# Two layers of sliding-window attention and token MLP on one core: the MLP's first product cut in five parts, the last attention chunk halved, masks moved to GpSimd

## The chip, the cores and the metric

The kernel runs on one core of a Trainium2 chip. A core has five engines that run side by side and wait for each other through semaphores: TensorE (PE; its weight loads are shown apart as PEld), VectorE (DVE), ScalarE (ACT), GpSimd (POOL) and SyncE (SP), which here issues every DMA. The metric is the device time of one execution in microseconds; smaller is better. The times before come from three runs.

## The reference

The input is x, 2048 rows of 512 numbers in bf16. Two kinds of block alternate, each added to x, twice over:

```python
def _A_ref(x, wqkv, wo):                      # sliding-window attention
    H = 32; Dh = D // H; W = 256              # 32 heads of 16
    ...
    scores = jnp.einsum("bhqd,bhkd->bhqk", q, k) * (Dh ** -0.5)
    mask = (idx[:, None] - idx[None, :] >= 0) & (idx[:, None] - idx[None, :] < W)
    p = _softmax(jnp.where(mask[None, None], scores, -1e9), axis=-1)
    ...
def _B_ref(x, w1, b1, w2, b2):                # MLP over the rows (tokens)
    h = _layernorm(x, axis=-1)
    u = _gelu(jnp.einsum("bsd,sf->bdf", h, w1) + b1)      # F = 1792
    y = jnp.einsum("bdf,fs->bds", u, w2) + b2
    ...
x = x + _A_ref(_layernorm(x, axis=-1), A_wqkv, A_wo)
x = x + _B_ref(_layernorm(x, axis=-1), B_w1, B_b1, B_w2, B_b2)
x = x + _A_ref(...)
x = x + _B_ref(...)
```

Each row attends to itself and the 255 rows before it. The token MLP's first product sums over all 2048 rows, so its sum can be finished only when the last rows have left the attention.

## The kernel before

Everything lies in on-chip memory in tiles of 128 partitions: x is 16 row tiles of 128 rows (`x_sb`), its normalised form is `xh_sb`. The work is written down as a list of operations (`op`), each with its engine, what it reads and what it writes; `Graph` derives the dependences. The order in which each engine gets its operations is not that of the list: it is a fixed, precomputed sequence (`ORDER`, unpacked by `begin_order` and laid out by `replay`), which also picks for some operations one of several engines (`alts`). Within one engine's queue, work runs strictly in this order. Buffers come from pools (`Pool`, `Tile`): a tile is taken at its first use and given back after its last, so a pool's size decides how early a later operation may start. `emit` writes the waits.

**Attention** works on chunks of query blocks of 64 rows (`CHUNKS`, as first block and number of blocks). For a chunk of 8 blocks and each of four groups of eight heads it makes five score units (`attention_plan`), for a chunk of 4 blocks five units for two groups together, one of them joint. A score unit is a set of small products of queries and spread keys (L710, line names as in the profile), four at a time in four strips of the array; then two exponentials on ACT over 128 x 1024 numbers (L736), which write the probabilities `pt` (seven buffers); then the masks; then the product with the values (L774), which takes three units, or two, or all five, at once. The sums of four head groups are turned on DVE (L794), divided (L798, L800), turned back (L805), multiplied with `wo` (L534) and added to x (L816).

The masks are applied in two ways. In most units GpSimd multiplies the finished probabilities with 0 or 1, as bit patterns (L757, made in `f_mask`). In layer 0, for the units listed in `BIASED` (in the chunk (4,4) the units 0 and 1, in (8,8) and (16,8) the units 2 and 4), PE adds a large negative number to the scores ahead of the exponential, with further small products of a selection matrix `sel` and a table `bb` (L721); these two are built at the start by twelve operations on DVE (L465, L472).

**Projections**: `qkv` turns the normalised rows of a chunk of 512 rows (four row tiles), multiplies them with `wqkv` (L534) and copies the results out of the accumulators: queries to `qT` (two buffers), keys over `stg` to `kbd` (three buffers, each for all four head groups; every second strip of 16 must be zero, cleared at the start by POOL, L482), values over `vst` and a DMA to `vb`.

**Token MLP**: the first product is accumulated in parts over row tiles. `PARTS` of layer 0 lists row tiles 0 to 3 (in the list after chunk (8,8)) and 4 to 11 (after chunk (24,8)), each for all 14 column tiles of 128; `u_part` makes them (L534, weights `w1b`, four buffers loaded by SP, L830), and DVE or ACT copies the first part's sums out (L880, L882), DVE adds the second's (L884). The last part, row tiles 12 to 15, is made by `u_last` (L895) after the attention, with the addition of the earlier sums on DVE (L906) and the activation on ACT (L910). A part starts only when its last row tile is there. Then `y_block` makes the second product row tile by row tile (L534, weights in `pt` and `w2b`), and its result goes to x (L936); in layer 0 these row tiles feed layer 1's projections.

At the start, `f_warm` issues 42 products of no use on PE while x is on its way (L395); then come the layer norm of the first row tiles (L492, L494, L505, L512), their turning on PE (L570, copied out at L579) and the first projections.

Of the kernel before, what the change touches and what calls it, by code (L numbers as in the profile page):

```python
# [15 lines left out]
    'c-p;HKZx_l6(4zLzti5$7bY-;K9~!0puiNmpaTUI(18Lf6i^|84jgdd!Urx~xX^(L6)IG?Foy~k3aD_QfD02`nBc;N3kO`daIuApEnIA|#THv^v4x9_*WO+4'  # L16
    '?zeYelH;ELNSb*wn)iFZ_j?rAF$R-hFaQl1MD2Rqc6z-ObQ9Q0I+5N0tsfxQJZ;LS!FS>l^i3OrI;cSnFmiiGyf&@5jmh6O=dO2NTm8i)OK$V|W~Nxg7^#NJ'
    'jjxzWMnhGW85~ZB!%dnDi#TCwz^U3X`=CE6K9r;3hd+J&A?k2$x9mn-Z`d_2@O-X0ys9W)ZDu~_p3arkO4F#KBpQtoqCinF!l<RHmyDTgyH(T%p_c@!H#fEo'
    'NVc*z7gx)rZQEqE`f@g-o6U?;v>FcifYR~k?(U8nMQON*e0lM;b<<dPEWE%=X9dwLoN9=Vo17!WSnl--R;v{`8+g1d*>cJ3@O|9YvQTV@`f(kFjD=AUgsre$'
    'mjA9V@Th3F+et!`s7Pp0q!H~kBfshgxY=lUp55>Wvn;<FRI61LU0q#Y-QCqLYZ$k#WABm}OV6p{>GYd_jSO=bcu3bBr;09vC~|ja!lu#fqK=_h3gbLjuXRIT'  # L20
    'a!#pfo0flZVL8syS+3A~GSdksh!<QHCs)g&$TCEfZLfz>#~TpkdUG||B%9m2+h+6bE_+|=tk>7K7_G*e%|()&uk6*#j?BWIPUot6bv2)_*K2Q>=l1z>B&XKg'
    'DyRL~yx;HJqp?r^Zjx_F+3)wVtoP?$-ox0o`(-~>Rof^i<(RQv7KT|Cwma9?##N_f7`!dZ?W!Eqo6V-Gaxd@!cT|~DS=Togx=zl|?Un7?OUKb<O`D9@OKwg$'
    '?qil?Sx)`T_iKsZPm=VbJa==KQf6B`HlsMHitSt~JG!h9g`8o_rj#1mnrfOxu!7Gf>dus*pyxPd;&??bw|cg!&;-S?5ow{JzsFe9G4C}pzhS5}U?O*xYML_R'
    '8dE5vf`XLl(`koLQ*e|6?M|uHY8uyded}y3Sw7SC1u$>c*Yh==&mq(h!o$<S_U>*7Zjp>Jl7)3rC=5s-ALRKKH=ENe&+`%3&7?8_zQ3WWtI8m5M2;{Bk^ngl'
    'u$o#GL7@4_b2+yR1^@)8FvHAj119Rkvcv#&b;cFWn8J346i_Hu$1|92=?jbMq~kh{m{1W|VJu$GCON?XqtwsUIE&-Bu4z#fQ4JHMAm5K7U*KTbwp9fHdjbMV'
    'm&;26=ks%@Y4&(V`NSIIdn>*ITkt_fc^F1#XR_REbUFyir@DR`*6Xz(2&&)LzpmFcSckGqF?3zzpPtDO%!F+@EEl#lzj2)5(CO6DG_BRTjYit&h(c>Sx^8M7'
    'htT&_)3FTz08v#!bO0e&i6l#g$OIN%rb*E4?d>%}NM9@#=bMcHSJj7;;dwe9t0PSt2wV$I^RnFc7(36h)k-OUTmGZk{ZU~GpbE0JQ?=wWjO%rs>)%n4GNv*Y'
    'Lc6t+<;M3LzFfBX`U0>1fEJ6AfmuFSET@ZtF)%La7=UrJ2}bqls8$1kBfBekI9yD1IoC9)>}SFOj}XB)>-O&;>=#KQb)_uIFt)O!i_H<nol=i1p%7CTg;_Q0'
    'R<c$%%i19boodag1MYfGvs(2;O5JL;&W8hs*K0x|8jS5K%drEYKECS%lQ^cR_49K_t6C6ZHqrg*G`PGBdIcD(*Ur_|KQ->yg7K=U8pdW5U)WKkYjLcGmTQS3'
    'Y1ok+;?~ubt{M98&jG)^k^R43se(cm4O(9<mkUbgA|q{8`Jnu6P>x0;H*hDO=eW~yOrW#SEK!i<e7-39L=mLw!SPO_I-R2YvUibQ;=EVIdEmO^F&=l_K~|=e'  # L30
    'h6%<7fr!}k_%@Dx&#hkgLCaq{#72&72SH5;RW)l?P1p5=*t%{IP=D)r)Kgs7kY)Ws5RZrsQC(8gFm6Xw9y_)xi(Uu?J2g!)Wzb@A+<>9RDO6~k)l{|sz?*Kj'
    'TQr#f{n{ZIsVtYNyqGT~!Twn~o6g`VoQy@F(QpU`Vdy2jZjx2{{Z<jhu4Q$_TV$gnhwUKsyk@<oyKW^-JvWKH7)Hp}bwg+m)OEpco3_~*L`|+jRfdoPfe^%w'
    'wS{mxxfBm~7Tv5j&AhAteYMi<RVrGaZjHw0<Kb#)>3Ugy^G%)`gP~}g3P_5qAU}XMwBN^;l{gDG-^oeXj^fDr_FLcgEVOZb&oSjc8W2DNA)>SZLZ?PIK;j7l'
    'Qr1ghFHL|@tDV{aAbYckswh+eghG(brY&u}U5oM(!bJiy8YAH(8b#T!*TsLm=vxM8Hd{?SYBZV+N-zYnnYeM1c1$OAfnkV3HUiVqEV+PyF;T;YX%Wj7osI~x'
# [59 lines left out]
class Graph:  # L94
# [4 lines left out]
    def __init__(self, nc, es):  # L99
        self.nc = nc  # L100
        self.sem = {e: es.enter_context(nc.semaphore(f"s_{e}")) for e in self.ENGS}
        self.dsem = [es.enter_context(nc.semaphore(f"s_dma{i}")) for i in range(self.NDMA)]
        self.ops = []
        self.last_w = {}
        self.readers = {}

    def op(self, eng, fn, reads=(), writes=(), cost=200.0, prio=None, dma=False, after=(), holds=(), cfg=None, cls=None,
# [20 lines left out]
        for k in writes:  # L128
# [3 lines left out]
            for rd in self.readers.get(k, ()):  # L132
                deps[rd.idx] = rd
# [882 lines left out]
```

## Time and profile before

| what | value |
|---|---|
| median of three runs | 444.22 us (443.94 to 444.88) |
| the profiled execution | 445.56 us, its span 443.6 us |
| granted TensorE clock, mean | 0.996 |
| PE busy | 418.5 us, 94% of the span |
| ACT busy | 322.7 us, 73% |
| DVE busy | 307.4 us, 69% |
| POOL busy | 201.1 us, 45% |
| masks on POOL (L757) | 226 operations, 146.9 us |
| mask products on PE (L721) | 352, from 21.7 to 117.0 us |

A span is what the profile sees between first and last instruction. A line of a group gives line number, engine, operation, what it writes and reads, the number of instructions, busy time and mean duration in ns, and then the idle time of the engine ahead of them, with what ended it. A line of a timeline gives start, length, engine, line and operation, the number of instructions merged in it, and in brackets the idle time ahead. The stages lie in time as follows: first exponential at 11.1 us; layer 0's attention to about 161; the end of the token MLP's first product to about 186; second product and layer 1's first projections to about 205; layer 1's attention to about 362; its first product to 392 and its second to the end. PE pipelines its products, so the busy time of a product contains a drain that lies under the next.

### The profile page before, as it was taken

How to read it: one execution, taken by the hardware profiler on the slowest of the kernel's cores; microseconds unless marked ns; L12 is line 12 of the kernel's file. 1: busy time of each engine (PE TensorE's matmuls, PEld its weight loads, DVE VectorE, ACT ScalarE, POOL GpSimd, SP SyncE). 2: the span in 40 equal slices, each digit the busy share in tenths (PEclk: the TensorE clock that was granted, in tenths of full speed). 3: DMA queues.
4: the chain of work that ended last, by engine and by line, in shares of the span. 5: the costliest groups of instructions: out<-in, count | busy, mean ns of one | idle time of the engine just before them, and what ended most of it. 6: DMA issues, size and time to landing. Idle time of an engine off the chain costs nothing.

```text
span 443.6 us, 14491 instructions
## 1 busy us (share of the span) xinstructions
PE 418.5 (94%) x6270; PEld 193.5 (44%) x6344; DVE 307.4 (69%) x582; ACT 322.7 (73%) x372; POOL 201.1 (45%) x305
## 2 busy tenths in 40 slices
PE   7888988998999999999999999999999999999997
PEld 5554443443443444444444444444334444444443
DVE  7988879777895678664468789898887457521223
ACT  3999999999999940708989999999999980430000
POOL 3567652464577641001456686677866551000000
PEclk8999999999999999999999999999999999999999
DMA  7575504410133538451434434031211347653533
GB/s 242 153 129 91 101 16 72 77 28 18 36 83 100 122 88 249 125 168 25 99 80 104 111 73 97 17 71 38 56 45 30 105 123 202 189 158 99 167 115 105
DMA packets 94127, 44.47 MB, mean 100 GB/s; under 512 B 24304, under 2 KB 94064, under 8 KB 94064
## 3 DMA queue, kind: packets, MB, share of 16 engines
q1 hardware_dynamic: 94064, 43.55, 39.1%
q8 instruction: 50, 0.82, 0.8%
q14 instruction: 13, 0.11, 0.1%
HBM read 33.56 MB, written 2.10 MB: 80 GB/s over the span
## 4 chain that ended last, share of the span: by engine, by line
PE 79%; ACT 13%; DVE 3%; issue 2%; DMA 1%; SPq 1%; POOL 1%; POOLq 0%
PE PS L534 53%; ACT pt L736 12%; PE PS L710 9%; PE PS L895 8%; PE PS L774 8%; DMA w1b<-in_B_w_dram 1%; DVE rl L794 1%; PE PS L721 1%; DVE stats L492 1%; SPq L830 1%; PE PS L570 0%; DVE vst L649 0%; DVE bb L472 0%; DVE x_sb L816 0%; POOL rstd L505 0%
## 5 line engine op out<-in xcount | busy, mean ns | idle before, releaser
L736 ACT ACTIVATE pt<-PS 128x1024 bf16<-128x1024 f32 (+1 forms) x304 | 281.9, 1034 | 12.0 <-PE PS L710 8.0
L757 POOL TENSOR_TENSOR pt<-pt,ldm 128x256 int32<-128x256 int32 (+2 forms) x226 | 146.9, 675 | 91.7 <-ACT pt L736 91.2
L534 PE MATMUL PS<-xhT,wqkv 128*128 128x512 bf16 (+1 forms) x267 | 65.3, 362 | 4.5 <-issue 1.4
L534 PE MATMUL PS<-xh_sb,w1b 128*128 128x512 bf16 x262 | 66.0, 380 | 2.9 <-issue 1.9
L534 PE MATMUL PS<-uT,w2b 128*128 128x512 bf16 (+1 forms) x285 | 66.7, 370 | 0.8 <-issue 0.5
L710 PE MATMUL PS<-qT,kbd 32*128 32x256 bf16 (+4 forms) x1488 | 60.4, 252 | 5.6 <-ACT pt L736 2.8
L936 DVE SCALAR_TENSOR_TENSOR x_sb<-PS,b2col,x_sb 128x512 bf16<-128x512 f32 x31 | 22.4, 745 | 48.4 <-PE PS L534 48.4
L505 POOL TENSOR_TENSOR rstd<-agg,mhalf 128x2 f32<-128x2 f32 (+1 forms) x33 | 23.5, 713 | 67.8 <-DVE agg L494 67.8
L794 DVE STREAM_TRANSPOSE rl<-PS 128x1024 f32<-128x1024 f32 x32 | 39.9, 1246 | 19.8 <-PE PS L774 19.3
L710 PEld LDWEIGHTS PS<-qT,kbd 32*128 32x128 bf16 x1488 | 22.0, 93 | 63.9 <-ACT pt L736 48.2
L774 PE MATMUL PS<-pt,vb 64*17 64x320 bf16 (+4 forms) x2976 | 43.6, 252 | 1.2 <-DVE vst L649 0.5
L910 ACT ACTIVATE uT<-rl,b1col 128x512 bf16<-128x512 f32 x28 | 18.5, 713 | 36.1 <-DVE rl L906 35.7
L492 DVE BATCH_NORM_STATS2 stats<-x_sb 128x6 f32<-128x512 bf16 x64 | 42.8, 678 | 0.4
L534 PEld LDWEIGHTS PS<-uT,w2b 128*128 128x128 bf16 x294 | 27.1, 98 | 30.9 <-issue 3.7
L534 PE MATMUL PS<-uT,pt 128*128 128x512 bf16 x163 | 39.5, 380 | 0.3
L774 PEld LDWEIGHTS PS<-pt,vb 64*17 64x17 bf16 x2976 | 31.0, 85 | 17.4 <-issue 7.3
L895 PE MATMUL PS<-xh_sb,w1b 128*128 128x512 bf16 x164 | 37.0, 379 | 0.7 <-DMA w1b<-in_B_w_dram 0.6
L534 PEld LDWEIGHTS PS<-xh_sb,w1b 128*128 128x128 bf16 x280 | 23.8, 98 | 31.6 <-issue 7.0
L534 PEld LDWEIGHTS PS<-xhT,wqkv 128*128 128x128 bf16 x288 | 24.5, 99 | 28.8 <-issue 5.6
L534 PE MATMUL PS<-wqkv,xhT 128*128 128x512 bf16 x115 | 32.3, 381 | 3.5 <-issue 1.3
L534 PE MATMUL PS<-wo_sb,oT 128*128 128x512 bf16 x124 | 32.6, 380 | 0.4 <-issue 0.3
L512 DVE TENSOR_SCALAR xh_sb<-x_sb,agg,rstd 128x512 bf16<-128x512 bf16 x64 | 27.2, 445 | 3.2 <-POOL rstd L505 3.1
(64 smaller groups left out, 337.0 us busy)
## 6 DMA issues: line engine op xcount, KB each, us to landing
w1b<-in_B_w_dram SPq DMA_DIRECT2D x112, 128.0 KB, 2.7
w2b<-in_B_w_dram SPq DMA_DIRECT2D x70, 128.0 KB, 2.6
pt<-in_B_w_dram SPq DMA_DIRECT2D x42, 128.0 KB, 3.2
vb<-vst SPq DMA_DIRECT2D x64, 68.0 KB, 2.1
out_dram<-x_sb SPq DMA_DIRECT2D x15, 128.0 KB, 1.8
x_sb<-in_A_x_dram SPq DMA_DIRECT2D x3, 512.0 KB, 7.3
wqkv<-in_A_wqkv_dram SPq DMA_DIRECT2D x4, 256.0 KB, 4.5
wqkv<-in_A_wqkv_dram SPq DMA_DIRECT2D x1, 512.0 KB, 6.6
```

The source lines that it names most:

```text
L492: op("vector:stat", lambda e: e.bn_stats(st[:, 0:6], x_sb[:, t, :]), reads=[f"x{t}"], writes=[("st", i)], cost=dve_cost(512))
L505: op("gpsimd:rstd", lambda e: e.tensor_tensor(rstd[:, t0:t1, 0], agg[:, t0:t1, 1], mhalf[:, 0:1].to_broadcast([P, t1 - t0]), op=ALU.pow), ...
L512: op("vector:xh", lambda e: e.tensor_scalar(xh_sb[:, t, :], x_sb[:, t, :], agg[:, t, 0:1], rstd[:, t, :], op0=ALU.subtract, op1=ALU.mult), ...
L534: return e.matmul(o, lhsT=w, rhs=x, start=start, stop=stop, skip_group_check=True)
L710: last = e.matmul(bank(tt[r // 2], r % 2)[:, base + c0 * 64:base + (c0 + n) * 64], lhsT=kbd[32 * r:32 * r + 32, tk.slot, o, jj].rearrange( ...
L736: op("scalar:exp", lambda e, ts=ts, tp=tp, i=i, cols=cols: e.activation(probs(tp)[:, i, 0:cols, :], pair(ts)[:, :, 0:cols].rearrange("p r ...
L757: return e.tensor_tensor(v, v, m, op=ALU.mult)
L774: last = e.matmul(bank(t, h)[32 * r:32 * r + 17, i + q0 * 64:i + (q0 + n) * 64], lhsT=vb[64 * h:64 * h + 64, tk.slot, jj, 4 * o + r, :], r ...
L794: op("vector:od", lambda e, t=tod, tr=tr: e.transpose(rl[:, tr.slot:tr.slot + 2].rearrange("p a b -> p (a b)"), pair(t)), reads=[(tod, i) ...
L895: last = e.matmul(bank(tu, tt), lhsT=v()[:, sc - b0, k0 + tt * P:k0 + (tt + 1) * P], rhs=xh_sb[:, sc, :], start=(sc == b0), stop=(sc == NT ...
L910: op("scalar:gelu", lambda e, ft=ft, tt=tt: e.activation(uT[:, ft, :], rl[:, tmps[tt].slot], ACTF.Gelu_apprx_tanh, bias=b1col[:, ft:ft + 1 ...
L936: op("vector:resy", lambda e: e.scalar_tensor_tensor(x_sb[:, t, :], bank(ft), b2col[:, t:t + 1], x_sb[:, t, :], op0=ALU.add, op1=ALU.add), ...
```

## The change

In layer 0:

- The last attention chunk of 8 query blocks becomes two of 4.
- The token MLP's first product is cut in five: row tiles 0 to 3 and 4 to 7 for all 14 column tiles; row tiles 8 to 11 for column tiles 0 to 7; row tiles 8 to 13 for column tiles 8 to 13; and the last part, row tiles 12 to 15 for column tiles 0 to 7 and row tiles 14 and 15 for column tiles 8 to 13 (`LAST`). Layer 1's cuts stay as they were.
- `BIASED` goes: all masks are applied by GpSimd, and `sel` and `bb` are no longer built.
- At the start, 40 warming products instead of 42, and after the turning of the first two row tiles 2 and 8 more (`keep_warm`), which the next operation on PE follows. The clearing of the key buffers by POOL (`zero_keys`) now waits for the second normalised row tile.

In both layers:

- The buffers of queries and keys are taken per head group (8 and 12 small ones in the place of 2 and 3 large ones, of the same total size), and the values have a pool of their own.
- `ORDER`, the sequence of all operations and the choice of engines, is another one; its text can't be read as such and is left out here.

```diff
+        if eng == "tensor":
+            after, self.next_pe = list(after) + self.next_pe, []
...
-    MASKED = 4e9
-    BIASED = [{1: (0, 1), 2: (2, 4), 3: (2, 4)}, {}]
-    CHUNKS = [[(0, 4), (4, 4), (8, 8), (16, 8), (24, 8)], [(0, 8), (8, 8), (16, 8), (24, 8)]]
-    PARTS = [[(2, 0, 4), (4, 4, 12)], [(2, 0, 8)]]
+    CHUNKS = [[(0, 4), (4, 4), (8, 8), (16, 8), (24, 4), (28, 4)], [(0, 8), (8, 8), (16, 8), (24, 8)]]
+    PARTS = [[(2, 0, 4, 0, 14), (3, 4, 8, 0, 14), (3, 8, 12, 0, 8), (4, 8, 14, 8, 14)], [(2, 0, 8, 0, 14)]]
+
+    LAST = [[(12, 0, 4), (14, 4, 7)], [(8, 0, 7)]]
...
-        qT = sb("qT", [P, 2, 4, 512])
+        qT = sb("qT", [P, 8, 512])
-        kbd = sb("kbd", [P, 3, 4, 8, 2, 64])
+        kbd = sb("kbd", [P, 12, 8, 2, 64])
...
-            for _ in range(42):
+            for _ in range(40):
...
+        def keep_warm(n, after):
+            spare = Tile(banks)
+
+            def f(e):
+                for _ in range(n):
+                    last = e.matmul(PS[:, spare.slot, 0:P], lhsT=uT[:, 0, 0:P], rhs=uT[:, 0, 0:P], start=True, stop=True)
+                return last
+            g.next_pe = [op("tensor:fw", f, reads=["uT0"], writes=[spare], cost=60 * n, cfg="f", cls="f", after=after)]
...
-        op("gpsimd:zero", lambda e: e.memset(sel[:].rearrange("p a b -> p (a b)").bitcast(dt.float32), 0.0), writes=["sel"], cost=200)
...
-            op("vector:sel", f_sel, reads=["ident", "sel"], writes=[("sel", r)], cost=150)
-            for i, (add, mul) in enumerate(((-1.0, MASKED), (0.0, -MASKED))):
...
-                op("vector:sel", f_bb, reads=["tri"], writes=[("bb", r, i)], cost=150)
...
-        for k in (1, 2):
-            op("gpsimd:zero", lambda e, k=k: e.memset(kbd[:, k].rearrange("p a b c d -> p (a b c d)").bitcast(dt.float32), 0.0),
-               writes=["kz0"], cost=1900)
...
+        def zero_keys():
+            for k in (1, 2):
+                op("gpsimd:zero", lambda e, k=k: e.memset(kbd[:, 4 * k:4 * k + 4].rearrange("p a b c d -> p (a b c d)").bitcast(dt.float32), 0.0),
+                   reads=["xh1"], writes=["kz0"], cost=1900)
...
-            tx, tq, tk = Tile(p_xhT), Tile(p_qT), Tile(p_kv)
+            tx, tq, tk, tv = Tile(p_xhT), [Tile(p_qT) for _ in range(4)], [Tile(p_k) for _ in range(4)], Tile(p_v)
...
+                if wide and not layer and m == 0:
+                    keep_warm((2, 8)[i], [g.ops[-1]])
...
+                if first and not layer:
+                    zero_keys()
...
-                    on_pe = su[0][0] in biased and len(su) == 1
...
-                        for c0, nc_, w0 in plan[su[0][0]][1] if on_pe else ():
-                            for a in range(2):
-                                lo = 32 if w0 < 2 and a else 0
-                                hi = nc_ * 64 - (32 if w0 + nc_ > 2 and not a else 0)
-                                for r in range(4):
-                                    last = e.matmul(
-                                        bank(tt[r // 2], r % 2)[:, c0 * 64 + lo:c0 * 64 + hi],
-                                        lhsT=sel[32 * r:32 * r + 32, a, :],
-                                        rhs=bb[32 * r:32 * r + 32, 1 - a].rearrange("p i n -> p (i n)")[:, w0 * 64 + lo:w0 * 64 + hi],
-                                        start=False, stop=True, tile_position=(32 * r, 0), skip_group_check=True)
...
-                    masks, mk = [] if on_pe else list(plan[su[0][0]][1]), []
+                    masks, mk = list(plan[su[0][0]][1]), []
...
-        def u_part(s0, s1, late):
-            nf = 2048 // (s1 - s0)
-            for f0 in range(0, F, nf):
-                tw, v = load_w1(s0, s1, f0, min(nf, F - f0), late)
-                for k in range(0, min(nf, F - f0), P):
+        def u_part(s0, s1, fa, fz, late):
+            nf = 2048 // (s1 - s0) // P * P
+            for f0 in range(fa * P, fz * P, nf):
+                tw, v = load_w1(s0, s1, f0, min(nf, fz * P - f0), late)
+                for k in range(0, min(nf, fz * P - f0), P):
...
-            for s0, s1 in [(s, s + 4) for s in range(b0, NT - 4, 4)] + [(NT - 4, NT - 2), (NT - 2, NT)]:
+            for s0, s1 in [(s, s + 4) for s in range(b0, NT - 4, 4)] + [(s, s + 2) for s in range(max(b0, NT - 4), NT, 2)]:
...
-                for c0, s0, s1 in PARTS[layer]:
+                for c0, s0, s1, fa, fz in PARTS[layer]:
-                        u_part(s0, s1, gate[c - 1])
+                        u_part(s0, s1, fa, fz, gate[c - 1])
...
-            c0, _, b0 = PARTS[layer][-1]
-            late = gate[c0 - 1]
-            nf = 2048 // (NT - b0)
-            w1t = {f0: load_w1(b0, NT, f0, min(nf, F - f0), late) for f0 in range(0, F, nf)}
...
+            late = [prev_sc[0]]
+            w1t = {}
+            for b0, fa, fz in LAST[layer]:
+                nf = 2048 // (NT - b0) // 256 * 256
+                for f0 in range(fa * 256, fz * 256, nf):
+                    w1t.update({fb: (b0, *t, fb * 256 - f0) for t in [load_w1(b0, NT, f0, min(nf, fz * 256 - f0), late)]
+                                for fb in range(f0 // 256, min(f0 + nf, fz * 256) // 256)})
...
-                k0 = fb * 256 % nf
-                u_last(fb, b0, *w1t[fb * 256 - k0], k0)
+                u_last(fb, *w1t[fb])
```

More of the change, by code (lines that the diff above doesn't have):

```diff
@@ L609, in proj @@
                     op(two[0][0] + ":evka", two[0][1], reads=[key] + [("par", h) for h in range(2)],
-                       writes=[(tk, "k", o, h, k) for h in range(2) for k in KEYS(a, b)], cost=two[0][2], prio=-3e5, alts=two[1:])
+                       writes=[(tk[o], h, k) for h in range(2) for k in KEYS(a, b)], cost=two[0][2], prio=-3e5, alts=two[1:])
                     if wide:
@@ L619, in f_kz @@
                     got = []
-                    assert layer or m > 2 or tk.slot
+                    assert layer or m > 2 or tk[o].slot > 3
                     for h in range(2):
@@ L955, in bass_interleave_layers__sliding_block__mixer_token_mlp__prompt_kernel @@
                 phase[0] = 8 * layer + c
-                tos[c] = attention(qs, nq, tqs, tks, BIASED[layer].get(c, ()))
+                tos[c] = attention(qs, nq, tqs, tks)
                 gate.append([prev_sc[0]])
```

118 lines of the change are left out of this document (50 added, 68 removed).

## The prediction

> **What bounds the kernel now.** I read the busy shares first, then the slices, then the stretches of layer 0 one by one, then single rows. The shares and slices name two engines:
>
> ```profile
> PE 418.5 (94%) x6270; PEld 193.5 (44%) x6344; DVE 307.4 (69%) x582; ACT 322.7 (73%) x372; POOL 201.1 (45%) x305
> PE   7888988998999999999999999999999999999997
> ACT  3999999999999940708989999999999980430000
> PE 79%; ACT 13%; DVE 3%; issue 2%; DMA 1%; SPq 1%; POOL 1%; POOLq 0%
> ```
>
> PE is full nearly everywhere; ACT is as full while the two attentions run (slices 1 to 13 and 18 to 32, counted from 0), and the chain of work that ended last is 79% PE. The view by windows (columns: window, length, then PE, PEld, DVE, ACT, POOL busy, clock, DMA) gives layer 0 by stage, and layer 1's attention in the last line:
>
> ```profile
> 5.06:11.00 5.94, 4.20 (x34) 2.52 (x34) 4.86 (x19) 2.63 (x6) 1.09 (x3) 0.71 1.00 310
> 17.00:47.00 30.00, 25.67 (x749) 14.80 (x754) 26.57 (x59) 28.18 (x34) 21.50 (x27) 1.00 0.58 93
> 47.00:86.00 39.00, 35.09 (x788) 16.09 (x796) 32.02 (x61) 38.00 (x41) 20.00 (x31) 1.00 0.38 72
> 86.00:122.00 36.00, 33.49 (x758) 15.20 (x764) 29.09 (x50) 35.27 (x39) 16.95 (x26) 1.00 0.12 29
> 122.00:160.70 38.70, 37.06 (x666) 15.94 (x673) 26.58 (x49) 36.38 (x40) 28.60 (x42) 1.00 0.36 87
> 160.70:186.00 25.30, 24.54 (x116) 11.14 (x117) 21.05 (x39) 7.64 (x12) 1.39 (x2) 1.00 0.66 184
> 205.00:360.00 155.00, 150.25 (x2504) 63.98 (x2533) 118.10 (x211) 147.82 (x168) 102.21 (x154) 1.00 0.29 71
> ```
>
> To be seen: from 17 to 122 PE idles 10.75 us of 105 (10.2%) while ACT is 97% full; from 122 PE idles 4% or less. So layer 0's attention ends when ACT's exponentials end (last around 158), and what PE has not done by then it does afterwards: after 160.7 come 31 products of the token MLP's middle part, 16 of the output projection and the 56 of its last part, at PE's own pace. Time is won where PE work goes away, or where it fills idle before 160.7.
>
> **The change, part by part.** All against the profiled execution: 445.56 us (span 443.6 and 1.96 around it); the median, 444.22, is 1.34 below.
>
> **1. Mask products leave PE.** 352 of them go, in 20 score units with 16 and 4 with 8 (chunk (4,4): four of each; chunks (8,8) and (16,8): eight of 16 each). Their price is the step from a unit's start to the next filler, with and without:
>
> ```profile
> 88.12 0.40 PE L710 MATMUL PS<-qT,kbd 32*128 32x64 bf16 x12
> 88.35 0.35 PE L721 MATMUL PS<-bb,sel 32*128 32x96 bf16 x16
> 88.64 1.04 PE L534 MATMUL PS<-xh_sb,w1b 128*128 128x512 bf16 x3
> 128.24 0.40 PE L710 MATMUL PS<-qT,kbd 32*128 32x256 bf16 x8
> 128.57 1.47 PE L534 MATMUL PS<-wo_sb,oT 128*128 128x512 bf16 x6
> ```
>
> 0.52 us with, 0.33 without: 0.19 each; the units with 8 take 0.42 (27.74 to 28.16): 0.09. 20 x 0.19 + 4 x 0.09 = -4.2 us. The other end is their whole busy time, 7.9 us; I take 4.2, because it is start to start and counts what PE gets back.
>
> **2. The same masks on POOL.** Per chunk of 8 blocks 36 operations instead of 20, for (4,4) 16 instead of 4, and the halved chunk has 32 instead of 36: +40. By form (743 ns for 128x256, 472 for 128x128, 996 for 128x384): 7.8 us in chunk (4,4), 11.9 in each of the two next, -2.1 in the last: +29.5 us of POOL. The rows of the covering pace:
>
> ```profile
> L757 POOL TENSOR_TENSOR pt<-pt,ldm 128x256 int32<-128x256 int32 x162 | 117.8, 743 | 57.4 <-ACT pt L736 56.8
> PEld PS L774 <- POOL pt L757: 3.1, 8, 0.5
> ```
>
> In all 226 masks PE waited 3.1 us for POOL, 14 ns each: 40 more cost +0.5 us. Bounds: 0 and the slower rival below. The stretch 122 to 160.7 already has every mask on POOL, and there PE idles least of the attention (4.2%); that is why I stay near the low end. Its cover is the seven probability buffers between exponential and value product; without it a mask's 0.74 us stands on the path each time.
>
> **3. The last chunk in halves.** Exponentials and score units stay 40 and 20, the columns too. A value product of 64 pieces takes 0.85 us (42.40 to 43.25), one of 96 takes 1.34 (131.34 to 132.68): 2 x 0.85 - 1.34 = 0.36, four times, 1.4. The four joint score units with 24 products take 0.41 instead of 0.33: 0.3. Together +1.7 us on PE (0.9 if a product's 0.14 us drain lies under the next). What it allows, the output projection of row tiles 12 and 13 before the attention ends, is in 4.
>
> **4. Five parts, and the new order.** The last part falls from 56 products to 8 x 4 + 6 x 2 = 44. A product costs 0.22 us:
>
> ```profile
> 172.16 9.01 PE L895 MATMUL PS<-xh_sb,w1b 128*128 128x512 bf16 x41 [0.55 <-DMA w1b<-in_B_w_dram]
> L884 DVE TENSOR_TENSOR w2b<-PS,w2b 128x512 f32<-128x512 f32 x7 | 4.7, 675 | 1.9 <-PE PS L534 1.9
> ```
>
> So 2.6 us move ahead of the attention's end. No product is saved: it pays only as far as PE idle there is filled. Before, row tiles 4 to 11 go as one part, needing tile 11, whose output projection ends near 130; after, tiles 4 to 7 are a part of their own, and theirs ends near 116. I can't read the order from the diff, so I bound it by idle shares: if 17 to 122 came down to the 4.2% of 122 to 160.7, 6.3 us are won; if the latter rose to 10.2%, 2.3 us are lost. I take -1.0: most idle before 122 is PE waiting for ACT, which more filler covers only in part. Added beside it: 14 more accumulations on DVE, 14 x 0.68 = 9.5 us, in PE's shadow while DVE has 30 us free between 17 and 160.7; without that cover PE would lack free banks. SP issues 55 weight loads instead of 56 of the same bytes (two of them 192 KB), at 0.47 us each: nothing; the only wait on one that PE showed is 0.55 us.
>
> **5. Start.** The eight products ahead of the first scores run at 228 ns (12 in 2.74 us from 7.60), later ones at 131 (8 in 1.05 from 12.50): up to -0.8 us if the ten filler products keep the clock, which is 0.71 in 5.06 to 11. They fill waits of 0.47 and 0.68 us; at 94 ns each the eight take 0.75, so up to +0.1. I take the middle, -0.4. The Trainium skill (TensorE: Matmul & The Clock Gate, "Part 1: The HAM clock gate") says that the full clock comes only after about 3.4 us of sustained activity, in a free-running window; the 0.71 agrees, and by that rule the sum would take -0.8, if the window falls well.
>
> **6. The rest.** The 3.6 us of clearing key buffers on POOL leave 16.7 and 29.7 and can lie in POOL's idle 4.85 us before 10.87; if not, they stay where they are: 0. Twelve small builds on DVE (2.7 us) go, all before 17 and between other work: 0. Buffers per head group come free sooner, in layer 1 too, where PE idles 4.75 us of 155: 0, at most -1.
>
> Sum: -4.2 + 0.5 + 1.7 - 1.0 - 0.4 = -3.4 us: 442.2 profiled, **440.8 on the median**.
>
> **Rivals.**
> *Idle is filled as well.* The early parts bring 17 to 122 to 4.2% idle: -6.3 in the place of -1.0, 435.5 us. For it: 56 products become available in 86 to 122. Against: DVE is 81% busy there and takes their evictions.
>
> *It goes nowhere.* The freed PE time lies where ACT sets the pace and becomes idle, as does what the halves add: -0.4 + 0.5, 444.3 us. For: ACT at 97%. Against: a backlog of 31 products after 160.7, so filler was short of room, not missing.
>
> *Slower: POOL and DVE become the bound in chunk (4,4).* Between 17 and 47 POOL would have 21.5 - 3.6 + 7.8 = 25.7 of 30 us and DVE has 26.57; over 17 to 160.7 the two rise from 201 to about 236 of 287 us, 82%, against 71% in layer 1's attention, the fullest shown without mask products. If the 7.8 us of added masks there stand uncovered, since only chunk (8,8)'s projections are ready as filler and these need DVE: 440.8 + 7.8 = 448.6 us. It decides once more than 3.4 of the 7.8 show. For it: operations of the two already stretch each other (the normalisation on DVE 316 ns at least, 406 median, 810 at most; masks 444, 726 and 1195). Against: 122 to 160.7. The Trainium skill (SBUF — State Buffer, "Who interferes with whom") says that GpSimd and certain VectorE operations take one shared port pair, the loser waiting for the whole instruction; those spreads agree, and by that rule the added masks hold up DVE too.
>
> **How the numbers follow.** Forecast 0.44, its own range 437.5 to 443.3; idle filled 0.14; nowhere 0.11; slower 0.31, since that load on the two engines is shown nowhere. 0.2% is 0.9 us, about what a measurement here tells from no change. Faster: 0.44 + 0.14 + 0.02 of the third; same: 0.08 of it; slower: 0.31 + 0.01. The range, 435 to 448.6, leaves out half of the slower case and a small part of the filled one.
>
> **What the profile after would show.** No L721 rows, masks near 266, and the step from a score unit to the filler at 0.33: step 1. POOL near 79% in 17 to 160.7, and waits of PE on POOL near 3.6 us in all: step 2. The last part with 44 products, first u activations sooner after the last exponential: step 4. PE idle in 17 to 122 at 9 to 10 us. Clock above 0.71 and the first exponential before 11.1: step 5. I am wrong if ACT shows gaps before 47 while masks queue on POOL, if PE waits on DVE's accumulations, or if layer 1, not named by any step, moves by more than 1 us.

## The result and the profile after

The kernel after takes 439.16 us (median, 438.71 to 439.51), the kernel before 444.4 us beside it. The ratio is 0.9881, with an interval of 0.9864 to 0.9898: 5.2 us faster, where 3.4 were forecast (440.8 us). The profiled execution took 438.96 us with a span of 437.2, which is 6.4 less than the span before; 1.3 of that is the one profiled execution of before, which lay that much above its median because of a low clock in its first microseconds.

The page of the kernel after: busy shares, the slices of PE and ACT, and the chain of work that ended last.

```profile
PE 415.4 (95%) x6120; PEld 189.4 (43%) x6192; DVE 307.8 (70%) x565; ACT 327.7 (75%) x382; POOL 238.0 (54%) x355
PE   8888999999999879999999999999999999999997
ACT  4999999999998971728999999999999971330000
PE 78%; ACT 11%; DVE 7%; issue 2%; DMA 0%; POOL 0%
```

The bound is the same: PE 95% busy, PE 78% of the chain. POOL has 37 us more work and DVE stands for 7% of the chain, before 3%. By stretches of layer 0 (window, length, then PE, PEld, DVE, ACT, POOL busy, clock, DMA), and layer 1's attention in the last line:

```profile
5.06:11.00 5.94, 5.33 (x69) 4.00 (x68) 5.41 (x18) 4.18 (x8) 1.20 (x3) 1.00 0.99 305
17.00:47.00 30.00, 26.27 (x648) 13.22 (x646) 28.45 (x57) 29.73 (x36) 27.04 (x38) 1.00 0.46 101
47.00:86.00 39.00, 37.55 (x669) 16.15 (x676) 33.58 (x62) 36.58 (x41) 32.32 (x49) 1.00 0.37 76
86.00:122.00 36.00, 34.88 (x657) 15.01 (x663) 29.98 (x53) 34.99 (x39) 28.63 (x42) 1.00 0.31 74
122.00:160.00 38.00, 34.40 (x762) 14.78 (x775) 33.19 (x58) 35.26 (x39) 24.84 (x36) 1.00 0.30 80
205.00:360.00 155.00, 149.83 (x2578) 64.40 (x2606) 112.32 (x197) 147.66 (x170) 112.19 (x167) 1.00 0.30 74
```

From 17 to 122 PE idles 6.30 us (3.73 + 1.45 + 1.12), before 10.75. In exchange POOL is at 90% in 17 to 47, DVE at 95%, ACT at 99%: three engines are nearly full at once. From 122 to the end of the attention PE idles more than before, 3.60 us for 1.64.

Where the time went is seen best from marks along the span, read from the timeline (us):

| | before | after | difference |
|---|---|---|---|
| start to first exponential | 11.1 | 9.0 | -2.1 |
| first to last exponential of layer 0 | 146.3 | 150.3 | +4.0 |
| last exponential to last gelu | 29.5 | 24.5 | -5.0 |
| last gelu to layer 1's first exponential | 20.1 | 17.7 | -2.4 |
| layer 1's first exponential to the end | 236.6 | 235.7 | -0.9 |

The marks are the starts of these operations. Of the first row 1.3 us is the clock: in the order of before, but with the clock at 1.00 in 5 to 11 us, the first exponential comes at 9.85 us (the run with the masks on GpSimd, below). The attention of layer 0 became longer, and the time was won behind it. The groups of instructions between the first and the last exponential show why; of before first, then of after (columns: count, busy us, mean ns of one, idle before them):

```profile
L534 PE MATMUL PS<-xh_sb,w1b 128*128 128x512 bf16 x118 | 30.6, 381 | 1.5 <-issue 1.1 <-ACT pt L736 0.3
L774 PE MATMUL PS<-pt,vb 64*17 64x320 bf16 (+4 forms) x1440 | 21.0, 249 | 1.1 <-DVE vst L649 0.5 <-POOL rstd L505 0.4 <-issue 0.2
L534 PE MATMUL PS<-wo_sb,oT 128*128 128x512 bf16 x46 | 12.6, 380 | 0.2 <-issue 0.2
L721 PE MATMUL PS<-bb,sel 32*128 32x96 bf16 (+2 forms) x352 | 7.9, 202 | 0.0
```

```profile
L522 PE MATMUL PS<-xh_sb,w1b 128*128 128x512 bf16 x147 | 39.1, 381 | 2.5 <-issue 1.6 <-DVE xh_sb L495 0.6 <-DVE uT L862 0.2
L752 PE MATMUL PS<-pt,vb 64*17 64x128 bf16 (+4 forms) x1536 | 21.3, 243 | 0.6 <-ACT pt L714 0.5
L522 PE MATMUL PS<-wo_sb,oT 128*128 128x512 bf16 x53 | 13.6, 380 | 0.5 <-issue 0.4
```

The mask products are gone (7.9 us busy), and 29 more products of the token MLP and 7 more of the output projection stand inside the attention. So what is left behind it falls from 103 products (31 + 16 + 56) to 68 (16 + 8 + 44): 35 x 0.22 = 7.7 us, nearly the 7.4 by which the way from the last exponential to layer 1's first became shorter (four more products of layer 1's projections stand there, 20 for 16). The freed PE time was neither won in place nor lost: it was filled with work from behind.

### The profile page after: what moved, and what is told of

The parts are those of the page before. It is cut to its first block, busy times and chain, and to the rows that moved or that the text cites. A ratio compares the mean times of both kernels' runs of the same rounds, so it can differ in the third digit from the quotient of the medians.

```text
span 437.2 us, 14225 instructions
## 1 busy us (share of the span) xinstructions
PE 415.4 (95%) x6120; PEld 189.4 (43%) x6192; DVE 307.8 (70%) x565; ACT 327.7 (75%) x382; POOL 238.0 (54%) x355
## 4 chain that ended last, share of the span: by engine, by line
PE 78%; ACT 11%; DVE 7%; issue 2%; DMA 0%; POOL 0%
PE PS L522 54%; ACT pt L714 11%; PE PS L699 9%; PE PS L873 8%; PE PS L752 7%; DVE rl L772 2%; DVE stats L475 1%; DVE xh_sb L495 1%; DVE kbd L593 1%; DVE qT L582 0%; DMA x_sb<-in_A_x_dram 0%; DVE uT L862 0%; DVE x_sb L794 0%; DVE vst L639 0%; POOL pt L735 0%
## 5 line engine op out<-in xcount | busy, mean ns | idle before, releaser
L735 POOL TENSOR_TENSOR pt<-pt,ldm 128x256 int32<-128x256 int32 (+2 forms) x266 | 176.4, 688 | 76.8 <-ACT pt L714 73.2
L522 PE MATMUL PS<-xh_sb,w1b 128*128 128x512 bf16 x267 | 69.2, 381 | 4.3 <-issue 2.6
L522 PE MATMUL PS<-uT,w2b 128*128 128x512 bf16 (+1 forms) x285 | 67.0, 369 | 0.8 <-issue 0.5
L522 PE MATMUL PS<-xhT,wqkv 128*128 128x512 bf16 (+1 forms) x275 | 64.9, 356 | 2.9 <-ACT pt L714 1.3
L699 PE MATMUL PS<-qT,kbd 32*128 32x64 bf16 (+4 forms) x1552 | 60.6, 247 | 5.3 <-ACT pt L714 2.2
L772 DVE STREAM_TRANSPOSE rl<-PS 128x1024 f32<-128x1024 f32 x32 | 39.8, 1244 | 17.7 <-PE PS L752 17.1
L699 PEld LDWEIGHTS PS<-qT,kbd 32*128 32x128 bf16 x1552 | 22.9, 92 | 64.0 <-ACT pt L714 45.9
L752 PE MATMUL PS<-pt,vb 64*17 64x128 bf16 (+4 forms) x3104 | 44.1, 248 | 2.1 <-ACT pt L714 1.0
L522 PEld LDWEIGHTS PS<-uT,w2b 128*128 128x128 bf16 x294 | 27.1, 98 | 31.0 <-issue 3.5
L522 PE MATMUL PS<-uT,pt 128*128 128x512 bf16 x162 | 39.9, 379 | 0.4 <-issue 0.2
L522 PEld LDWEIGHTS PS<-xh_sb,w1b 128*128 128x128 bf16 x292 | 23.6, 97 | 32.8 <-issue 7.2
L522 PEld LDWEIGHTS PS<-xhT,wqkv 128*128 128x128 bf16 x288 | 24.3, 97 | 29.9 <-issue 6.1
L873 PE MATMUL PS<-xh_sb,w1b 128*128 128x512 bf16 x153 | 34.9, 379 | 0.2
L495 DVE TENSOR_SCALAR xh_sb<-x_sb,agg,rstd 128x512 bf16<-128x512 bf16 x64 | 30.5, 501 | 4.7 <-POOL rstd L488 4.6
L522 PE MATMUL PS<-wqkv,xhT 128*128 128x512 bf16 x119 | 32.3, 381 | 0.9 <-issue 0.6
L522 PE MATMUL PS<-wo_sb,oT 128*128 128x512 bf16 x121 | 31.0, 380 | 1.1 <-issue 0.6
```

Of the source, the lines that this page charges most:

```text
L495: op("vector:xh", lambda e: e.tensor_scalar(xh_sb[:, t, :], x_sb[:, t, :], agg[:, t, 0:1], rstd[:, t, :], op0=ALU.subtract, op1=ALU.mult), ...
L522: return e.matmul(o, lhsT=w, rhs=x, start=start, stop=stop, skip_group_check=True)
L699: last = e.matmul(bank(tt[r // 2], r % 2)[:, base + c0 * 64:base + (c0 + n) * 64], lhsT=kbd[32 * r:32 * r + 32, tk[0][o].slot, jj].rearran ...
L735: return e.tensor_tensor(v, v, m, op=ALU.mult)
L752: last = e.matmul(bank(t, h)[32 * r:32 * r + 17, i + q0 * 64:i + (q0 + n) * 64], lhsT=vb[64 * h:64 * h + 64, tk[1].slot, jj, 4 * o + r, :] ...
L772: op("vector:od", lambda e, t=tod, tr=tr: e.transpose(rl[:, tr.slot:tr.slot + 2].rearrange("p a b -> p (a b)"), pair(t)), reads=[(tod, i) ...
```

## The experiments

The times are medians; the kernel before ran beside each, at 444.4 to 444.7 us, and after is 439.16. In the profiles of the kernels that share the start of after, the first exponential comes at 9.0 to 9.7 us although nothing differs there, so a difference of less than 0.7 us between two profiles says little.

### Masks: the old order with them on GpSimd

```
-    BIASED = [{1: (0, 1), 2: (2, 4), 3: (2, 4)}, {}]
+    BIASED = [{}, {}]          # kernel before; each new mask right behind its unit's second exponential
```

> The kernel before with one part of the change alone: no unit is masked on PE, the 44 masks that take the place of the mask products are put into GpSimd's queue right behind the unit's second exponential; order, chunks and parts of the MLP as before, and the twelve small builds on DVE stay. By steps 1 and 2 of the prediction: -4.2 + 0.5 = -3.7, 440.7 us. Rival 'it goes nowhere' (the freed PE time lies where ACT sets the pace): 444.4 within 0.9 us. Rival 'POOL and DVE become the bound in chunk (4,4)': above 446, with waits of PE on masks and gaps on ACT between 17 and 47 us.

471.41 us, ratio 1.0606 (1.0584 to 1.0627): 27 us slower. Its waits between 17 and 60 us, then PE's timeline, then POOL's:

```profile
ACT pt L735 <- PE PS L709: 9.8, 7, 5.6
PEld PS L773 <- POOL pt L756: 7.9, 2, 5.4
```

```profile
31.81 0.40 PE L709 MATMUL PS<-qT,kbd 32*128 32x192 bf16 x12
37.45 1.26 PE L773 MATMUL PS<-pt,vb 64*17 64x64 bf16 x64 [5.24 <-POOL pt L756]
39.47 0.61 PE L709 MATMUL PS<-qT,kbd 32*128 32x64 bf16 x24 [0.76 <-DVE stg L613]
```

```profile
32.97 1.05 POOL L799 TENSOR_TENSOR ul<-rl,rc 128x512 bf16<-128x512 f32 x1
33.96 1.80 POOL L481 MEMSET kbd<- 128x2048 f32 x1
35.72 1.67 POOL L756 TENSOR_TENSOR pt<-pt,ldm 128x256 int32<-128x256 int32 x2
```

PE's queue is in strict order: a value product that waits for a mask keeps back the score units behind it, and then ACT has nothing to exponentiate (7 waits, the longest 5.6 us). Chunk (4,4) takes 27.2 us instead of 20.0, chunk (8,8) 49.0 instead of 39.0. After the 5.24 us of waiting PE runs slower as well: a value product of 64 pieces takes 1.26 us instead of 0.84, at a granted clock of 0.50. The waits of the slower rival are real, at its place and dearer than it priced them. But its reason, too much load, is not what this run shows: POOL is busy 19.96 of the 30 us from 17 to 47. During the wait it works off a division (1.05 us) and the clearing of a key buffer (1.80 us), and only then the masks for which PE waits. So what costs here looks like the place of the masks in POOL's queue rather than its load; the two were not tested apart.

### Masks: the new order with them back on TensorE

```
-                    masks, mk = list(plan[su[0][0]][1]), []
+                    masks, mk = [] if on_pe else list(plan[su[0][0]][1]), []   # and the 352 products, sel and bb
```

> The changed kernel with the masks of the same units of chunks (4,4), (8,8) and (16,8) back on PE as mask products (352 of them), the 44 masks gone from GpSimd, and the two small tables built on DVE after the fourth normalised row tile; order otherwise as it is. If steps 1 and 2 hold here as well: +3.7, 442.9 us. If GpSimd's added load is what makes the attention of the changed kernel longer (its exponentials end 151.4 us after the first one, before 147.4): the attention gets shorter by up to 4 us and the total stays at 439 or falls below it. If neither counts: 439.2 within 0.9.

449.6 us, 1.0119 (1.0105 to 1.0133): 10.4 us over after, above all three values of the expectation. But 3.3 us of it arise in the first chunk, where the twelve small builds, put behind the fourth normalisation, keep DVE from the first query evictions. So the builds were put where before has them:

> As the kernel with the masks back on PE, but with the two tables built where the kernel before builds them, at the very start, so that the first chunk is not held up by them (it was: its exponentials took 14.5 us instead of 11.2). If the 6.2 us that chunks (4,4), (8,8) and (16,8) lost there are the mask products' own price: 439.2 + 6 to 7 = 445.5 us. If that loss followed from the late start: 442.9 us, step 1 and 2 as predicted. The first exponential would show what the twelve small builds cost at the start: at 9.0 to 9.3 nothing, at 9.9 (the kernel before, where the clock held) 0.6 to 0.9 us.

450.79 us, 1.0135 (1.0118 to 1.0152), above both values. Its profiled execution started late (first exponential at 12.5 us, clock 0.77 in 5 to 11). The three chunks that hold the masks, from their first exponential to the next chunk's, take 20.4, 44.8 and 40.7 us; in after they take 19.2, 40.5 and 38.9. That is 7.3 us, in the first of the two kernels 6.2. But these hold a halt in chunk (8,8) that is no mask product: one value product of 96 pieces stops ahead of its last two, for 2.16 us here and 2.44 in the first kernel, and waits for nothing that the profile shows ("issue"). In after the same value product runs through:

```profile
58.53 1.36 PE L791 MATMUL PS<-pt,vb 64*17 64x64 bf16 x94
62.06 0.31 PE L791 MATMUL PS<-pt,vb 64*17 64x320 bf16 x2 [2.16 <-issue]
```

```profile
52.69 1.41 PE L752 MATMUL PS<-pt,vb 64*17 64x64 bf16 x96
```

From the start of the two exponentials around it to the next one it takes 5.66 and 5.09 us, in after 3.03. Without these 2.6 and 2.1 us the masks on PE cost 4.7 and 4.1 us; in the 4.7 is also a clock of 0.78 and 0.87 in the 10 us from 60 on, while in the first kernel it was 1.00 there. Steps 1 and 2 together had 3.7. By chunk it is 1.2 us in (4,4) and 1.8 in (16,8), where step 1's price from start to start gives 1.1 and 1.5. What caused the halt is open; the kernel before, with the same mask products, has none. The order was planned without these products, so this is their price in this order.

### Masks: how much room GpSimd has

```
+                            if more:             # 12 masks of chunk (4,4)
+                                w_ = scr[:, nm, :, 0:reps * w].rearrange("p a (b c) -> p a b c", b=reps)
+                                e.tensor_tensor(w_, v, m, op=ALU.mult)
                             return e.tensor_tensor(v, v, m, op=ALU.mult)
```

> The kernel after, with a second GpSimd operation of the same size ahead of each of the 12 masks of chunk (4,4) that stood on TensorE before; it writes a scratch buffer, and the result is unchanged. It doubles the suspected load of the slower rival at its place: about 12 x 0.65 us = 7.8 us more on GpSimd, which was busy 27.0 of 30 us between 17 and 47 us. Theory (GpSimd there has hardly room left, the new order only just covers the masks): +4 to +8 us, chunk (4,4) longer by that much, and PE or ACT waits on masks L735 that the kernel after doesn't show. Rival (the seven probability buffers and the lag of the value products cover it): within 1 us of 439.2.

446.77 us, 1.0047 (1.0033 to 1.0061): 7.6 us over after for 7.7 us of added work (8 x 728 ns + 4 x 466 ns). Windows and PE's timeline of this kernel:

```profile
17.00:47.00 30.00, 23.50 (x480) 11.04 (x481) 23.73 (x47) 24.78 (x30) 29.10 (x43) 0.89 0.37 78
34.70:38.30 3.60, 0.01 (x2) 0.00 (x1) 3.06 (x5) 1.46 (x2) 3.60 (x7) 0.89 0.18 36
38.30:42.40 4.10, 3.77 (x88) 1.62 (x89) 2.27 (x3) 1.94 (x2) 4.10 (x7) 0.50 0.72 130
42.40:44.30 1.90, 1.90 (x9) 0.73 (x6) 0.86 (x2) 1.79 (x2) 1.90 (x4) 0.50 0.06 13
44.30:47.00 2.70, 2.57 (x24) 0.74 (x22) 2.68 (x2) 1.96 (x3) 2.70 (x5) 0.99 0.00 0
```

```profile
34.10 0.60 PE L522 MATMUL PS<-xhT,wqkv 128*128 128x512 bf16 x2
38.30 1.26 PE L758 MATMUL PS<-pt,vb 64*17 64x64 bf16 x64 [3.59 <-POOL pt L741]
```

POOL is full (29.10 of 30 us). One value product waits 3.59 us, and for the next 6 us the granted clock is 0.50: PE pays for the wait and then again for the way back. The same doubling in chunk (16,8), where POOL was busy 28.6 of 36 us:

> The kernel after, with the same doubling as after_masks_twice_44 moved to chunk (16,8): 12 of its 36 masks (eight of 128x256, four of 128x128) each preceded by a second operation of its size that writes a scratch buffer; the result is unchanged. That is about 8 x 0.73 + 4 x 0.53 = 8.0 us more on GpSimd, where it is busy 28.6 of 36 us. Theory (what counts is whether GpSimd has room over the chunk; the probability buffers cover a single mask): room 7.4 us, so 0.6 us stands out at least, +0.5 to +3 us, 439.7 to 442.2. Rival (each mask lies on the path, however much room there is): +7 us or more, as in chunk (4,4), where 7.7 us more cost 7.6: 446 or above.

441.34 us, 0.9915 (0.9901 to 0.9929): 2.2 us over after. POOL rises to 35.7 of 38 us, no wait of PE on a mask there is above 1.4 us, and the clock stays at 1.00:

```profile
86.00:124.00 38.00, 35.36 (x663) 14.76 (x664) 30.55 (x54) 35.22 (x39) 35.70 (x54) 1.00 0.34 72
PEld PS L758 <- POOL pt L741: 1.7, 2, 1.4
```

Both fit POOL's room over the chunk. From a chunk's first exponential to the next chunk's, POOL is busy 18.43 of 19.20 us in chunk (4,4) of after and 30.33 of 38.90 in (16,8): with 0.8 us of room 7.7 more cost 7.6, with 8.6 us of room some 8 more cost 2.2. These are two points in two chunks, and part of the 7.6 is the slow clock. The kernel after runs close to the edge in chunk (4,4).

### The cut: twelve products back behind the attention

```
-  mm_group("fu", ft, s1 - s0, lambda ...
+  mm_group("fu", ft, 4 if s0 == 8 else s1 - s0, lambda ...
+  # u_last: the products of row tiles 14 and 15 twice where the part holds these two alone
```

> The changed kernel with the 12 products that the new cut moves ahead of the attention's end put back behind it: for column tiles 8 to 13 the part over row tiles 8 to 13 sums over 8 to 11 only, and the last part takes row tiles 14 and 15 twice over, so that row tiles 12 and 13 are left out of these columns' sums. Loads, waits and order stay. Theory (step 4: the moved products fill idle PE time, and the tail is PE's own pace): 12 x 0.22 = 2.6 us more in the tail and nothing won ahead of it: 441.8 us. Rival (PE is as full ahead of the attention's end as behind it, so the place of a product does not matter): 439.2 within 0.9. Step 4's own figure, a part of it paying, would be 440.2.

441.64 us, 0.9936 (0.9923 to 0.9948): 2.5 us over after, against 12 x 0.22 = 2.6. The attention takes 149.3 us instead of 150.3, and from the last exponential to the last gelu 27.6 instead of 24.5. The products that step 4 moved pay almost in full; it had counted 1.0 for all of them.

### The cut: the old parts in the new order

```
-    PARTS = [[(2, 0, 4, 0, 14), (3, 4, 8, 0, 14), (3, 8, 12, 0, 8), (4, 8, 14, 8, 14)],
-    LAST = [[(12, 0, 4), (14, 4, 7)],
+    PARTS = [[(2, 0, 4, 0, 14), (5, 4, 12, 0, 14)],
+    LAST = [[(12, 0, 7)],
```

> The changed kernel with the MLP's first product cut as before (row tiles 0 to 3, 4 to 11, and 12 to 15 after the attention, each for all column tiles); the halved last chunk, the masks on GpSimd and the order of everything else stay. The products of row tiles 4 to 11 take the places that the changed order gives to such products after row tile 11 is normalised (38 of 62 places, 30 of them ahead of the attention's end); 36 products are left behind the last value product, before it were 31. Theory (step 4 is the main gain: the 48 products that the changed order runs ahead of row tile 11 fill idle, beside the 12 of the tail): 2.5 for the 12, as measured, and 2 to 4 for the filler missing ahead of row tile 11: 443.5 to 446 us. Rival (early availability of row tiles 4 to 7 is worth nothing, the rest of the order keeps PE full): 441.7 us.

455.42 us, 1.0232 (1.021 to 1.0253): 16.3 us over after, beyond both values. Its windows:

```profile
86.00:122.00 36.00, 29.95 (x637) 12.24 (x636) 24.87 (x46) 35.42 (x41) 28.63 (x43) 0.95 0.20 41
122.00:161.00 39.00, 33.66 (x710) 13.70 (x708) 27.24 (x49) 35.51 (x39) 25.25 (x36) 1.00 0.28 71
```

PE idles 6.05 us in 86 to 122, in after 1.12, while ACT keeps its pace (35.4 us); what didn't find a place waits behind the attention, where the last exponential to the last gelu takes 37.5 us instead of 24.5. There PE's timeline has 52 products of the middle part, where the expectation had 36, and the last part's 56: 48 more than in after, 48 x 0.22 = 10.6 us, and with a wait of 2.6 us for weights this is the 13 us. So row tiles 4 to 7 as a part of their own are the filler for the stretch before. How much of the 16.3 us is the cut itself stays open, since the products had to be placed by hand.

### The halves of the last chunk

```
-    CHUNKS = [[(0, 4), (4, 4), (8, 8), (16, 8), (24, 8)],
+    CHUNKS = [[(0, 4), (4, 4), (8, 8), (16, 8), (24, 4), (28, 4)],
```

In the kernel before, unit for unit in the old places:

> The kernel before with one part of the change alone: chunk (24,8) as (24,4) and (28,4). The 20 score units and exponentials and the eight value products take the places of the old ones, the masks (32 in the place of 36) stand behind their unit's second exponential, and the output projection and layer norm of row tiles 12 and 13 stand behind the first half. Step 3: +1.7 us on PE, less what the earlier output projection gives back: 446.1 us, if nothing is given back. Rival (the tail behind the attention is PE's own pace and the added PE time lies under ACT's): 444.4 within 0.9 us.

466.95 us, 1.0504 (1.0481 to 1.0526). And the reverse, in the new order, from the kernel with the twelve products moved back (in both, row tiles 12 and 13 are left out of the column tiles 8 to 13 of the product, and 14 and 15 are counted twice):

> The kernel after_12_back (12 products of the first MLP product in the tail, of the last row tiles alone) with the last chunk of layer 0 in one piece again, (24,8) in the place of (24,4) and (28,4), every unit in the place of one of the halves' units; row tiles 12 and 13 are projected and normalised together with 14 and 15. It stands against after_12_back, 441.6 us. Theory (step 3: the halves cost about 1.7 us of PE while the attention runs, and bring 8 projection products of 0.23 us and two normalisations ahead of its end): the last exponential comes 1 to 2 us sooner, the tail is 2 to 5 us longer, 441.5 to 445 us in all. Rival (the halves are dear, as the kernel before with halves alone suggests): faster than 440.6. Second rival (the whole chunk upsets the queues as the halves did in the order of before): above 447.

461.76 us, 1.0388 (1.0365 to 1.0411), 20 us over after_12_back. Both lie far from the prices that they were to tell apart; the second where its rival of upset queues had it. PE's timeline of the first kernel, then of the second, behind its last value product:

```profile
136.67 0.40 PE L708 MATMUL PS<-qT,kbd 32*128 32x256 bf16 x8 [1.41 <-POOL kbd L627]
138.20 0.61 PE L708 MATMUL PS<-qT,kbd 32*128 32x192 bf16 x12 [1.13 <-ACT pt L734]
138.74 5.92 PE L532 MATMUL PS<-xh_sb,w1b 128*128 128x512 bf16 x14
144.83 4.49 PE L532 MATMUL PS<-xh_sb,w1b 128*128 128x512 bf16 x20 [0.17 <-DVE uT L882]
150.19 0.41 PE L708 MATMUL PS<-qT,kbd 32*128 32x64 bf16 x24 [0.88 <-DVE kbd L627]
```

```profile
163.91 1.04 PE L751 MATMUL PS<-pt,vb 64*17 64x64 bf16 x40 [1.71 <-POOL pt L734]
168.60 5.73 PE L521 MATMUL PS<-wo_sb,oT 128*128 128x512 bf16 x15 [3.64 <-DVE oT L782]
179.26 5.78 PE L521 MATMUL PS<-xh_sb,w1b 128*128 128x512 bf16 x16 [4.93 <-DVE xh_sb L494]
```

In the first, 34 MLP products bunch up ahead of a score unit, and ACT waits 9.8 us. In the second all row tiles of the chunk go through projection and normalisation at once behind the attention, and PE has nothing beside them: it waits 3.64 and 4.93 us, and runs the products between at half speed (15 in 5.73 us, 382 ns each, for some 220). What the halves allow is filler for these gaps. Their own price isn't settled by these two; the rows of value products above (21.0 to 21.3 us busy inside the attention; to the end of the MLP's first product 22.4 to 23.0) put it below the 1.7 us of step 3.

### Keep-warm products, buffers, layer 1

Without the ten filler products:

```
-                if wide and not layer and m == 0:
-                    keep_warm((2, 8)[i], [g.ops[-1]])
```

> The changed kernel without the 2 + 8 products on PE after the first two turned row tiles; all else, the order too, as it is. Theory (the products keep the clock, and a later first exponential is paid in full, since PE and ACT are both full from there on): the first twelve products of the projections go from 1.48 us back to about 2.7, the first exponential from 8.96 us to about 10.2, and the end moves by as much: 439.2 + 1.2 = 440.4 us. Rival (a start that is only 1 us later is absorbed by the waits of the first 40 us): the clock drops all the same, but the end moves by less than 0.4 us. By the prediction's step 5 (0.4) the two can't be told apart; by its upper end (0.8) it would be 440.0.

439.21 us, 0.9886 (0.9871 to 0.9902): no difference. The clock in 5 to 11 us is 1.00 without them too; the drop that theory and rival both assumed did not come.

Buffers alone, in the kernel before:

```
-        qT = sb("qT", [P, 2, 4, 512])
+        qT = sb("qT", [P, 8, 512])             # kbd alike; one buffer per head group, same order of work
```

> The kernel before with the key and query buffers given out per head group, and nothing else: the same operations in the same order. Theory (step 6: the buffers bring nothing by themselves, what they change is what the order may do): 444.4, within 0.9 us. Rival (buffers that come free sooner shorten waits of the projections by themselves): 443.4 or less, with the gain in layer 1's attention or in 17 to 122 us.

444.22 us, 0.9992 (0.998 to 1.0005): nothing by themselves.

Layer 1, from its first score unit on, in before's order and on before's engines:

> The changed kernel with everything from layer 1's first score unit on in the relative order (and on the engines) that the kernel before has; layer 0 and the projections ahead of that unit as they are. From that unit to the end the kernel before takes 236.6 us and the changed one 235.7. If that 0.9 us is the order's: 440.1 us. If it is the buffers per head group (which stay here) or chance: 439.2 within 0.9 us. Step 6 expected nothing from layer 1.

441.32 us, 0.992 (0.9903 to 0.9938): 2.2 us over after, more than either value. In the profile the way from the last gelu to layer 1's first exponential is 0.8 us longer and layer 1 from there 0.8, together 1.6; the rest lies ahead of it, where nothing was changed. So 1.6 to 2.2 us of the gain lie in a layer to which the sum gave nothing.

## Why the prediction was right, and where its steps were not

The direction, the mechanism (PE work goes away or moves ahead of the attention's end) and the size within 1.8 us were right. That the sum came so near is in part luck. What could be measured alone is 4.1 us for steps 1 and 2 (3.7 in the sum), 2.5 for twelve products of step 4 (1.0 for all of it), 1.6 to 2.2 for layer 1 (nothing) and nothing for step 5's products (0.4). These make more than the 5.2 us of the whole; they are prices within the new order and don't add up, and step 3 has none.

**Step 1** (-4.2). The rows came as forecast: no L721, 266 masks, and 0.33 us from score unit to filler in a chunk that had 0.52 (timeline of after):

```profile
50.01 0.40 PE L699 MATMUL PS<-qT,kbd 32*128 32x192 bf16 x8
50.34 1.90 PE L522 MATMUL PS<-wo_sb,oT 128*128 128x512 bf16 x8
```

Put back, the products cost 4.1 to 4.7 us net of the masks that leave GpSimd, without the halt in chunk (8,8); 1.2 and 1.8 us in the two other chunks, for 1.1 and 1.5 by the step's price. So the argument that only start to start counts held; the other end, 7.9, is not borne out.

**Step 2** (+0.5). POOL is at 79% from 17 to 160 us (112.8 of 143), as forecast, and the three forms lasted 736, 487 and 999 ns (743, 472 and 996 before). The waits were forecast too small: PE's weight loads wait for masks 7.4 us in the whole kernel, where 3.1 us before and 3.6 after were put down. In layer 0 it is 0.7 before and 3.1 after (lines of before, of after, and of after over the whole kernel); PE itself waits 0.7 us there, before not at all:

```profile
PEld PS L774 <- POOL pt L757: 0.7, 2, 0.4
PEld PS L752 <- POOL pt L735: 3.1, 6, 1.2
PEld PS L752 <- POOL pt L735: 7.4, 16, 1.2
```

The rest of the growth lies in layer 1, whose 136 masks are the same. What the waits cost in time was not measured apart from step 1. "Its cover is the seven probability buffers" was only half of it. The same buffers didn't cover the masks in the old order, nor twelve more in chunk (4,4). The cover is room on POOL, and an order in which value products stand where their masks are done. The slower rival named the right place: 7.7 us of added work there cost 7.6.

**Step 3** (+1.7). Not settled. By busy time +0.3 to +0.6 us on the value products; the attention's last stretch, (24,8) or its halves, is 2.1 us longer than before, but holds more filler.

**Step 4** (-1.0) is the term that was mis-sized most. Twelve products alone are worth 2.5, and 35 fewer products stand behind the attention in all. PE idle in 17 to 122 came to 6.3 us, not to 9 or 10: 4.45 less than before, of which 1.96 more idle from 122 to the attention's end take back nearly half. The rival "idle is filled as well" wanted 4.4 us of idle in 17 to 122; the 435.5 that it priced didn't come, and the attention became 4.0 us longer. The last part shows the forecast 44 products (43 recorded), and the first u activation follows the last exponential's end by 12.9 us, before by 17.8. DVE covered the 14 more accumulations: in the attention PE's MLP products idle 0.2 us for them (the row of L522 above).

**Step 5** (-0.4) failed. The clock was 1.00 and the first exponential came at 9.0 us, both as the step wanted, but the kernel without the filler products does the same (9.3 us, 1.00), and the second kernel with the masks back on PE, which has them, shows 0.77 after a wait of 2.06 us ahead of them. The clock of 0.71 in the one execution of before was taken for a property of the kernel: the same order had 1.00 in another run, and its first exponential at 9.85 us. What makes the rest of the start, 0.2 to 0.9 us, was not tested. The rule cited there, on sustained activity (the Trainium skill, TensorE: Matmul & The Clock Gate, "Part 1: The HAM clock gate"), isn't refuted: the filler products just didn't decide it.

**Step 6** (0, at most -1). Right for the buffers alone. Wrong for layer 1, by the sign that the prediction named itself: 1.6 to 2.2 us hang on its new order. In the windows from the last gelu to its first exponential PE is full in both kernels (19.98 of 20.10 us before, 17.59 of 17.70 after) with 110 and 100 products recorded. The ones that are gone belong to the MLP's second product (27 of its products with `pt` for 41) and were done ahead of the last gelu; of layer 1's projections there are four more ahead of the first score unit, 20 for 16. With before's order of layer 1 in the kernel after it would be eight more, 24: four products of 0.22 us over after, about the 0.8 us by which that way became longer there.

## What to carry to other kernels

Where PE is full and the order is written out, ask of each freed stretch which work can be ready for it: here the gain was made behind the attention, because parts became ready early enough to fill it. An operation that moves to another engine is paid by that engine's room over the chunk in question, and by the order: the same masks on GpSimd cost 27 us in the old order, and the whole change with the new order gains 5. The price of one part taken out of such a bundle is a price within that order; the parts don't add up.

## What was not expected of the hardware

**A wait of PE costs twice.** After 3.59 us without work the clock was granted at 0.50 for 6 us (38.3 to 44.3 us, in the windows above of the kernel with doubled masks in chunk (4,4)). Four products of 512 columns took 1.89 us in that time, elsewhere 1.03, and a value product of 64 pieces 1.26 instead of 0.84. The Trainium skill (TensorE: Matmul & The Clock Gate, "Why this matters for your kernels") advises against idle gaps of PE above some 3 us, and these rows agree. But no single long gap is needed: in the kernel before with halves alone PE worked 1.50 us of 4.70, in pieces with no wait above 1.41 us, and the clock fell to 0.53 for the next 6 us, while PE was busy throughout:

```profile
134.00:138.70 4.70, 1.50 (x22) 0.52 (x22) 3.08 (x8) 1.58 (x2) 2.45 (x4) 0.87 0.51 140
138.70:144.60 5.90, 5.90 (x20) 1.90 (x14) 0.52 (x1) 2.19 (x3) 1.86 (x3) 0.53 0.00 0
144.80:149.30 4.50, 4.47 (x20) 1.88 (x20) 2.51 (x5) 0.00 (x0) 0.00 (x0) 1.00 0.42 117
```

What a slow clock took can be estimated from above, as the span times what the mean granted clock lacks of 1: 0.033 x 469.8 = 15.5 us of the 27 with the masks on GpSimd in the old order (where PE also waited 19.8 us for masks), 0.022 x 466.3 = 10.3 of the 22 with the halves alone, 0.026 x 459.2 = 11.9 of the 20 of the reverse, but only 0.004 x 451.8 = 1.8 of the 16 with the old cut.

**DVE's normalisation became slower**, from a mean of 445 to 501 ns over 64 operations, 3.6 us in all. In layer 0 (17 to 165 us) it follows the masks on POOL: 397 ns before, 422 and 425 with the masks back on PE in the new order, 470 in after, 530 with the doubled masks in chunk (4,4). But in layer 1 it rose as well, from 472 to 543 ns, with the same masks; so their number is not all of it, and that the two engines share a port was not tested.
